# Retention attention and a Mish MLP on one core: state product on quarters of the array, scores moved behind the output ahead of them, state summed in SBUF, layer-2 tiles whole

## The chip, the cores and the metric

The kernel runs on one core of a Trainium2 chip. Times are device microseconds (us). "Time" is that of the whole execution; "span" is from the first to the last instruction in the profile and is about 1.7 us shorter. PE is TensorE's matmul side, PEld its weight loads, DVE is VectorE, ACT is ScalarE, POOL is GpSimd.

## The reference

```python
# q, k, v: (8, 8, 576, 64), that is batch, heads, sequence, head size
gamma  = 1.0 - 2.0 ** (-5.0 - np.arange(H))
Dmat   = np.where(rel >= 0, gamma[:, None, None] ** rel, 0.0)     # rel = i - j
ret    = (q @ k.T / sqrt(D)) * Dmat @ v
x      = ret.transpose(0, 2, 1, 3).reshape(4608, 512)
h      = x @ w_in                                                 # 512 -> 2048
out    = (h * tanh(softplus(h))) @ w_out                          # Mish, 2048 -> 512
```

Attention without a softmax can be done in chunks: within 128 positions by masked scores, across chunks by a state, the sum of k times v of all earlier positions (64 by 64 a head).

## The kernel before

There are 36 chunks of 128 positions in 18 pairs; four chunks make one of nine token tiles, 0 to 8, for the MLP. Pairs 0 and 1 and the chunks 4 to 7 (pairs 2 and 3) are handled chunk by chunk while the loads come in; pairs 4 to 7 with transposes on PE among the first layer-2 work; from pair 8 on DMA transposes q and k, and the rhythm is steady. The parts that the argument touches:

```python
ps_sc = ... bufs=2   # scores, 2 banks each     ps_st = ... bufs=1   # running state
ps_h  = ... bufs=2   # layer 1                  ps_o  = ... bufs=1   # layer 2

def step_k(m):       # add this pair to the state, which stays in PSUM
    ...
        nc.tensor.matmul(st[ds(64 * e, 64), u, p, :], lhsT=ks[:, u, h, :], rhs=vs[:, u, h, :], ...)
    for e in range(2):                       # two casts: a block-diagonal copy, zeros beside each head
        nc.scalar.activation(ssb[:, :, :, e, :], st, AX.Copy, scale=diag[:, e:e + 1])

def step_o(n):
    ot = sc[:, 0]
    ...      # across: 128 rows deep, half of them zeros, 64 columns
        nc.tensor.matmul(ot[ds(64 * e, 64), p, ...], lhsT=st_sb[b, i0][:, p, e, :], rhs=qk[:, 0, u, p, ...], ...)
    ...      # within: v times masked scores
        nc.tensor.matmul(ot[ds(64 * e, 64), p, :], lhsT=vs[:, u, 2 * p + e, :], rhs=sm[:, e, p, :], ...)
    (nc.scalar.copy if t == 0 else nc.vector.tensor_copy)(xts[t][:, :, ts(s, P)], ot)

# steady loop, 8 steps a pair: step 0 scores, step 4 state and outputs; g1 = 4 matmuls, g2 part = 4 matmuls
            if w == 0:   one(n, "S"); one(n + 1, "S"); step_p(m + 1); step_v(m + 1)
            elif w == 4: step_k(m); one(n, "O"); one(n + 1, "O")
            g1(t, i)
            g2(t - 1, i)
```

## Time and profile before

| | before |
|---|---|
| time, median of the first 3 runs | 317.01 us (316.92 to 317.5) |
| span of the profiled run | 315.1 us |
| PE busy | 97% |
| 512-column layer-1 and layer-2 matmuls | 496 and 560, 0.216 us each where they follow one another |
| a pair of chunks in the steady part | 15.84 us, 2.03 of them attention |

PE is the bound, so the way to read this profile is to ask what PE's own stream is made of. It helps to cut the span at three instructions: the first 512-column layer-1 matmul, the first layer-2 (G2) matmul, and the first layer-1 matmul of token tile 2. Here is the busy time of each engine in the four stretches, in the order start, chunk by chunk, PE transposes, rest. The columns are the stretch, its length, and the busy time of PE, PEld, DVE, ACT and POOL.

```profile
core 0: us, PE busy (x) PEld busy (x) DVE busy (x) ACT busy (x) POOL busy (x), PEclk, DMA share, GB/s
0.00:23.94 23.94, 19.52 (x159) 9.38 (x160) 14.44 (x35) 12.14 (x23) 20.13 (x36) 1.00 0.81 182
23.94:58.36 34.42, 33.31 (x497) 25.26 (x498) 13.77 (x18) 22.82 (x37) 21.25 (x23) 1.00 1.36 212
58.36:85.91 27.55, 27.36 (x276) 14.25 (x274) 15.28 (x17) 8.23 (x11) 11.93 (x13) 1.00 1.45 224
85.91:315.10 229.19, 225.71 (x1713) 110.26 (x1711) 90.74 (x103) 83.11 (x137) 30.89 (x37) 1.00 0.60 112
```

The reader is to see that the last stretch is three quarters of the time and nearly all PE, and that in the second ACT is busy for two thirds (22.82 of 34.42): there other engines are not far from setting the pace.

### The profile page before, as it was taken

The numbers are of one execution on the slowest core, as the hardware profiler recorded it, in microseconds if no ns is written. First come the engines' busy times: TensorE is split into PE (matmuls) and PEld (weight loads), VectorE is DVE, ScalarE is ACT, GpSimd is POOL, SyncE is SP. The second block draws the span as 40 slices with busy tenths as digits, with TensorE's granted clock in tenths as the row PEclk, the third lists the DMA queues.
The fourth block names the chain that finished last, engine by engine and source line by source line (L and its number), as shares of the span: only waits on it lengthen the run. The fifth ranks groups of instructions, "written<-read, shape, count | busy, mean of one in ns | idle before, by whom it ended". The sixth has DMA issues, their size and how long they took to land.

```text
span 315.1 us, 6075 instructions
## 1 busy us (share of the span) xinstructions
PE 305.9 (97%) x2639; PEld 159.2 (51%) x2639; DVE 134.2 (43%) x173; ACT 126.3 (40%) x208; POOL 84.2 (27%) x106
## 2 busy tenths in 40 slices
PE   7899999999999999999999999999999999999995
PEld 2355589645555544444545454445454545444444
DVE  4932463048649282626262626262626232001011
ACT  4556666322455642343434343434343432333300
POOL 6897672543340403131404040500000000000000
PEclk9999999999999999999999999999999999999999
DMA  6899999999999695959797969793131400000032
GB/s 170 240 134 219 206 205 220 201 229 253 198 251 166 127 132 108 197 110 201 158 141 157 142 139 160 165 149 87 46 89 45 91 33 35 33 33 35 33 83 83
DMA packets 71946, 43.38 MB, mean 138 GB/s; under 512 B 55664, under 2 KB 63088, under 8 KB 71920
## 3 DMA queue, kind: packets, MB, share of 16 engines
q0 software_dynamic: 43424, 26.22, 55.8%
q1 hardware_dynamic: 28352, 16.65, 20.4%
q8 instruction: 20, 0.33, 0.5%
q10 hardware_dynamic: 144, 0.13, 0.1%
q14 instruction: 6, 0.05, 0.0%
HBM read 36.70 MB, written 9.44 MB: 146 GB/s over the span
## 4 chain that ended last, share of the span: by engine, by line
PE 91%; DVE 4%; ACT 1%; DMA 1%; SPq 1%; issue 1%; DVEq 0%
PE hp L369 34%; PE ops L407 32%; PE hp L407 6%; PE hp L392 4%; PE sc L305 3%; PE sc L354 3%; PE sc L347 2%; PE st L326 2%; DVE qks L236 2%; PE sc L284 2%; PE hp L419 1%; DVE sm L308 1%; DMA qraw<-in_q_dram 1%; SPq L138 1%; ACT qkT L285 1%; PE hp L380 1%
## 5 line engine op out<-in xcount | busy, mean ns | idle before, releaser
L369 PE MATMUL hp<-xT,w_in_t 128*128 128x512 bf16 x496 | 126.5, 380 | 0.7 <-ACT gT L394 0.7
L371 ACT ACTIVATE gT<-hp 128x512 bf16<-128x512 f32 x124 | 74.1, 598 | 126.9 <-PE hp L369 126.6
L407 PE MATMUL ops<-w_out_t,gT 128*128 128x512 bf16 x480 | 121.9, 379 | 0.0
L407 PEld LDWEIGHTS <-gT 128*128 128x128 bf16 x560 | 54.2, 98 | 64.7 <-issue 0.8
L427 DVE COPY res<-ops 128x512 f32<-128x512 f32 x30 | 20.8, 692 | 128.0 <-PE ops L407 128.0
L369 PEld LDWEIGHTS <-w_in_t 128*128 128x128 bf16 x496 | 46.0, 98 | 53.8 <-DMA w_in_t<-in_moe_w_in_dram 0.8
L308 DVE TENSOR_TENSOR sm<-sc,mask 128x1024 bf16<-128x1024 f32 x36 | 42.6, 1217 | 20.2 <-PE sc L305 20.2
L540 POOL COPY seen<-qkT 1x1 bf16<-1x1 bf16 x10 | 1.8, 177 | 124.9 <-DMA qkT<-qks 124.9
L330 ACT ACTIVATE ssb<-st,diag 128x512 bf16<-128x512 f32 x32 | 20.2, 684 | 15.3 <-PE st L326 15.3
L358 DVE CAST xT<-sc 128x512 bf16<-128x512 f32 x32 | 20.8, 686 | 5.3 <-PE sc L354 4.5
L107 POOL DMA_DIRECT2D qraw<-in_q_dram x16 | 17.2, 1076 | 15.2 <-DVE qks L240 7.1
L257 DVE TENSOR_TENSOR vs<-vraw,gv 128x1024 bf16<-128x1024 f32 (+1 forms) x18 | 19.8, 1101 | 0.0
L240 DVE TENSOR_TENSOR qks<-qraw,gq 128x1024 bf16<-128x1024 f32 (+1 forms) x18 | 19.7, 1097 | 0.0
L107 POOL DMA_DIRECT2D qks<-in_k_dram x16 | 17.2, 1079 | 8.3 <-DMA qraw<-in_q_dram 3.8
L107 POOL DMA_DIRECT2D vraw<-in_v_dram x16 | 17.3, 1087 | 6.3 <-DMA w_out_t<-in_moe_w_out_dram 2.2
L407 PE MATMUL hp<-w_out_t,gT 128*128 128x512 bf16 x80 | 18.8, 380 | 0.0
L285 ACT COPY qkT<-sc 128x1024 bf16<-128x1024 bf16 x12 | 12.1, 1014 | 11.7 <-PE sc L284 11.7
L392 PE MATMUL hp<-xT,w_in_t 128*128 128x128 bf16 x272 | 16.7, 220 | 0.0
L392 PEld LDWEIGHTS <-w_in_t 128*128 128x128 bf16 x272 | 15.4, 98 | 0.7 <-issue 0.2
L354 PE MATMUL sc<-sm,vs 128*64 128x128 bf16 x288 | 13.9, 220 | 0.6 <-DVE sm L308 0.5
L305 PEld LDWEIGHTS <-qkT 64*128 64x128 bf16 x288 | 8.1, 94 | 10.2 <-issue 5.5
L305 PE MATMUL sc<-qkT 64*128 64x128 bf16 x288 | 11.9, 218 | 1.3 <-ACT qkT L285 0.8
(68 smaller groups left out, 157.1 us busy)
## 6 DMA issues: line engine op xcount, KB each, us to landing
out_dram<-res SPq DMA_DIRECT2D x31, 256.0 KB, 3.1
qraw<-in_q_dram POOLq DMA_DIRECT2D x12, 512.0 KB, 8.2
vraw<-in_v_dram POOLq DMA_DIRECT2D x12, 512.0 KB, 9.3
vraw<-in_v_dram POOLq DMA_DIRECT2D x12, 256.0 KB, 7.3
qks<-in_k_dram POOLq DMA_DIRECT2D x12, 256.0 KB, 8.5
qraw<-in_q_dram POOLq DMA_DIRECT2D x8, 256.0 KB, 9.4
w_out_t<-in_moe_w_out_dram POOLq DMA_DIRECT2D x4, 512.0 KB, 12.0
qraw<-in_q_dram SPq DMA_DIRECT2D x8, 128.0 KB, 4.0
```

What stands on the lines that cost most here:

```text
L107: nc.gpsimd.dma_start(out=t[ds(off, ni)].rearrange("p u h d -> p (u h) d"), in_=src[ds(b, 2), :, ds(i0, ni), :].rearrange("b h p d -> p (b ...
L257: (nc.gpsimd if early else nc.vector).tensor_tensor(r["vs"][:, u], r["v"][:, u], g, op=OP.mult)
L305: nc.tensor.matmul(sc[:, e, p, :], lhsT=qk[r, 1, u, p, :], rhs=qk[r, 0, u, p, :], start=True, stop=True)
L308: nc.vector.tensor_tensor(sm.rearrange("p e n i -> p (e n) i"), sc.rearrange("p e n i -> p (e n) i"), (mask if len(chunks[n]) == 1 else ma ...
L330: nc.scalar.activation(ssb[:, :, :, e, :], st, AX.Copy, scale=diag[:, e:e + 1])
L354: nc.tensor.matmul(ot[ds(64 * e, 64), p, :], lhsT=vs[:, u, 2 * p + e, :], rhs=sm[:, e, p, :], start=(start and p == 0), stop=True, skip_gr ...
L358: (nc.scalar.copy if t == 0 else nc.vector.tensor_copy)(xts[t][:, :, ts(s, P)], ot)
L369: nc.tensor.matmul(hp, lhsT=w_in_t[:, c, ts(f, P)], rhs=xts[t][:, c, :], start=(c == 0), stop=(c == KC - 1))
L371: nc.scalar.activation(gts[t][:, f, :], hp, AX.Mish)
L392: nc.tensor.matmul(hp[:, j, :], lhsT=w_in_t[:, c, ts(4 * fb + j, P)], rhs=xts[t][:, c, ts(s, P)], start=(c == 0), stop=(c == KC - 1))
L407: nc.tensor.matmul(ops, lhsT=gts[t][:, f, ts(s, P)], rhs=w_out_t[:, f, :], start=(f == 0), stop=(f == nF - 1))
L427: copy(ot, ops)
```

## The change

The intent: make PE's attention work shorter. The state product uses 64 by 64 quarters of the array, four at once; the scores of the next pair follow the output of the pair ahead, so that PE leaves its full shape once a pair and not twice. Three two-bank tiles for the scores make that possible, so the banks of the running state and of layer 2 go: the state is summed in SBUF by DVE, and a layer-2 tile is computed whole, in the banks of layer 1. Heads are regrouped (h and h + 4 share rows), and the decay moves from v to k, as DVE must now reorder k in any case.

```diff
-    ps_sc = ... bufs=2    ps_st = ... bufs=1    ps_o = ... bufs=1
+    ps_sc = ... bufs=3
 def step_p(m, ...):                       # DVE, once for each chunk
-        qks[:, 0] = q * gq                # k came by DMA as bf16; step_v: vs = v * gv
+        qks[:, 0] = q * gq;  qks[:, 1] = k * gk      # v comes by DMA as bf16
 def step_k(m):
+        if m < 6: st = ps_sc.tile(...)    else: st = ps_h.tile(...)
+        nc.vector.tensor_tensor(st_sum[b], st_sum[b], st, op=OP.add)      # or a copy, for the first
-        for e in range(2): nc.scalar.activation(ssb[..., e, :], st, AX.Copy, scale=diag[:, e:e + 1])
+        nc.scalar.copy(ssb, st_sum[b])
 def across(n, ot):
-        nc.tensor.matmul(ot[ds(64 * e, 64), p, ...], lhsT=st_sb[b, i0][:, p, e, :], rhs=qk[:, 0, u, p, ...])
+        r, p = ds(64 * e, 64), 2 * g + c
+        nc.tensor.matmul(ot[ds(64 * c, 64), e, g, ...], lhsT=st_sb[b, i0][r, p, :], rhs=qk[r, 0, u, p, ...])
 def step_o(n):                            # single chunks
-        (nc.scalar.copy if t == 0 else nc.vector.tensor_copy)(xts...)
+        within(...); across(...); nc.scalar.copy(xt...)
+def pair_o(m):                            # both chunks into the second one's score tile
+        step_k(m); within(u=0); within(u=1); across(u=0); across(u=1)
+        nc.vector.tensor_copy(xt..., sc...)          # one copy, 128x1024
 # steady loop
-            if w == 0: scores(m) ...   elif w == 4: step_k(m); outputs(m)
-            g1(t, i); g2(t - 1, i)
+            g1(t, i)
+            if i % 4 == 3:
+                if w == 7: pair_o(m); scores(m + 1)
+                for j in range(4): g2(t - 1, i - 3 + j)
```

Layer-2 tiles from token tile 2 on are copied out by ACT, and the transposes of pairs 6 and 7 by DVE.

More of the change, by code (lines that the diff above doesn't have):

```diff
@@ L75 @@
     PS = bass.MemoryType.PSUM
-    ps_sc = ctx.enter_context(tc.tile_pool(name="ps_sc", bufs=2, space=PS))
-    ps_st = ctx.enter_context(tc.tile_pool(name="ps_st", bufs=1, space=PS))
+    ps_sc = ctx.enter_context(tc.tile_pool(name="ps_sc", bufs=3, space=PS))
     ps_h = ctx.enter_context(tc.tile_pool(name="ps_h", bufs=2, space=PS))
-    ps_o = ctx.enter_context(tc.tile_pool(name="ps_o", bufs=1, space=PS))
     ctx.enter_context(tc.manual_schedule())
@@ L89, with by_slots @@
     w_out_r = moe_w_out.rearrange("(f p) d -> p f d", p=P)
+    def by_slots(x):
+        return x.rearrange("p (s r) d -> p r s d", r=2)
     def load(m):
@@ L93, in load @@
             return
-        qr = io.tile([P, 2, H, D], F32, name="qraw")
-        vr = io.tile([P, 2, H, D], F32, name="vraw")
-        qks = io.tile([P, 2, 2, H, D], BF16, name="qks", bufs=6)
-        pairs[m] = {"q": qr, "v": vr, "qks": qks, "ks": qks[:, 1]}
+        r = pairs[m] = {}
+        r["q"] = io.tile([P, 2, H, D], F32, name="qraw")
+        r["k"] = io.tile([P, 2, H, D], F32, name="kraw")
         if m < NCH // 2:
-            kr = io.tile([P, 2, H, D], F32, name="kraw", bufs=NCH // 2)
-            pairs[m]["k"] = kr
+            r["v"] = io.tile([P, 2, H, D], F32, name="vraw", bufs=NCH // 2)
             return
+        r["vs"] = tok.tile([P, 2, H, D], BF16, name="v", bufs=5)
         if m < NCH:
             return
-        for t, src in ((qr, q), (qks[:, 1], k), (vr, v)):
+        for x, src in (("q", q), ("k", k), ("vs", v)):
             off = 0
@@ L107, in load @@
                 nc.gpsimd.dma_start(
-                    out=t[ds(off, ni)].rearrange("p u h d -> p (u h) d"),
+                    out=r[x][ds(off, ni)].rearrange("p u h d -> p (u h) d"),
                     in_=src[ds(b, 2), :, ds(i0, ni), :].rearrange("b h p d -> p (b h) d"))
@@ L116, in load_single @@
         b, i0, _ = chunks[n][0]
-        r = pairs[m]
-        for t, src in ((r["q"], q), (r["qks"][:, 1], k), (r["v"], v)):
-            nc.gpsimd.dma_start(out=t[:, u], in_=src[b, :, ds(i0, P), :].rearrange("h p d -> p h d"))
+        for x, src in (("q", q), ("k", k), ("vs", v)):
+            nc.gpsimd.dma_start(out=pairs[m][x][:, u], in_=src[b, :, ds(i0, P), :].rearrange("h p d -> p h d"))
     def load_w_in(f, nf):
@@ L135, in load_first @@
         for x, src in (("q", q), ("k", k)):
-            heads = src.rearrange("b (p e) s d -> b e p s d", e=2)
+            heads = src.rearrange("b (e p) s d -> b e p s d", e=2)
             for e in range(2):
@@ L151, with scores_tile @@
     nc.vector.memset(idle, 0.0)
-    warm = ps_o.tile([P, d_model], F32, name="ops")
+    ahead = []
+    def scores_tile():
+        return ahead.pop() if ahead else ps_sc.tile([P, 2, NP, P], F32, name="sc")
     def keep_warm(n):
+        ahead.append(scores_tile())
         for _ in range(n):
-            nc.tensor.matmul(warm, lhsT=idle[:, 0:P], rhs=idle, start=True, stop=True)
+            nc.tensor.matmul(ahead[0][:, 0].rearrange("p n i -> p (n i)"), lhsT=idle[:, 0:P], rhs=idle, start=True, stop=True)
     keep_warm(11)
@@ L182 @@
             nc.vector.tensor_scalar(own[:, e, a:a + 1], off1, float(a),
-                                    math.log(1.0 - 2.0 ** (-5.0 - 2 * a - e)), op0=OP.is_equal, op1=OP.mult)
+                                    math.log(1.0 - 2.0 ** (-5.0 - a - 4 * e)), op0=OP.is_equal, op1=OP.mult)
     lg1 = consts.tile([P, 2], F32)
@@ L195 @@
     gq = consts.tile([P, 5, H], F32)
-    gv = consts.tile([P, 5, H], F32)
-    nc.scalar.activation(gv, ex, AX.Exp, scale=-1.0)
+    gk = consts.tile([P, 5, H], F32)
+    nc.scalar.activation(gk, ex, AX.Exp, scale=-1.0)
     nc.scalar.activation(gq, ex, AX.Exp)
@@ L210 @@
     load_v(1)
-    diag = consts.tile([P, 2], F32)
-    nc.vector.memset(diag, 0.0)
-    nc.vector.memset(diag[0:64, 0:1], 1.0)
-    nc.vector.memset(diag[64:P, 1:2], 1.0)
     seen = consts.tile([1, 1], BF16)
-    st_ps = {}
+    st_sum = {}
     st_sb = {}
@@ L229, in by_lines, with scale_first, cast_first @@
         return x.rearrange("p (t e) d -> p e t d", e=2)
-    def step_p(m, u0=0, nu=2):
+    def scale_first(n):
+        m, u = divmod(n, 2)
         r = pairs[m]
-        u = ds(u0, nu)
-        if m < NCH // 2:
-            nc.vector.tensor_tensor(by_lines(r["qks"][:, 0, u0]), by_heads(r["q"][:, u0]),
-                                    gq1.unsqueeze(3).to_broadcast([P, 2, 4, D]), op=OP.mult)
-            return
-        g = gq[:, place(2 * m), :].unsqueeze(1).unsqueeze(3).to_broadcast([P, nu, H, D])
-        nc.vector.tensor_tensor(r["qks"][:, 0, u], r["q"][:, u], g, op=OP.mult)
-    def step_c(n):
+        if u == 0:
+            r["qks"] = io.tile([P, 2, 2, H, D], BF16, name="qks")
+            r["vs"] = tok.tile([P, 2, H, D], BF16, name="v1", bufs=NCH // 2)
+        nc.vector.tensor_tensor(by_lines(r["qks"][:, 0, u]), by_heads(r["q"][:, u]),
+                                gq1.unsqueeze(3).to_broadcast([P, 2, 4, D]), op=OP.mult)
+    def cast_first(n):
         m, u = divmod(n, 2)
@@ L246, in step_c, with decay_first, step_p @@
         nc.gpsimd.tensor_copy(by_lines(r["qks"][:, 1, u]), by_heads(r["k"][:, u]))
-    def step_v(m, u0=0, nu=2):
+    def decay_first(n):
+        m, u = divmod(n, 2)
         r = pairs[m]
-        u = ds(u0, nu)
-        early = m < NCH // 2
-        if "vs" not in r:
-            r["vs"] = (tok.tile([P, 2, H, D], BF16, name="vs1", bufs=NCH // 2) if early
-                       else tok.tile([P, 2, H, D], BF16, name="vs"))
-        g = gv[:, place(2 * m), :].unsqueeze(1).unsqueeze(3).to_broadcast([P, nu, H, D])
-        (nc.gpsimd if early else nc.vector).tensor_tensor(r["vs"][:, u], r["v"][:, u], g, op=OP.mult)
+        nc.gpsimd.tensor_tensor(r["vs"][:, u], r["v"][:, u],
+                                gk[:, place(n), :].unsqueeze(2).to_broadcast([P, H, D]), op=OP.mult)
+    def step_p(m, us=(0, 1)):
+        r = pairs[m]
+        if "qks" not in r:
+            r["qks"] = io.tile([P, 2, 2, H, D], BF16, name="qks")
+            r["ks"] = r["qks"][:, 1]
+        for u in us:
+            for i, (x, g) in enumerate((("q", gq), ("k", gk))):
+                nc.vector.tensor_tensor(
+                    by_slots(r["qks"][:, i, u]), r[x][:, u].rearrange("p (r s) d -> p r s d", r=2),
+                    g[:, place(2 * m), :].rearrange("p (r s) -> p r s", r=2).unsqueeze(3).to_broadcast([P, 2, NP, D]),
+                    op=OP.mult)
     def step_t(n):
@@ L284, in step_t @@
                 nc.tensor.transpose(tp[:, i, p, :], flat[:, ts(p, P)], ident)
-        nc.scalar.copy(r["qk"][:, :, u], tp)
+        (nc.vector.tensor_copy if m in (6, 7) else nc.scalar.copy)(r["qk"][:, :, u], tp)
     def step_n(m):
@@ L300, in step_s @@
         qk = pairs[m]["qk"]
-        sc = ps_sc.tile([P, 2, NP, P], F32, name="sc")
+        sc = scores_tile()
         for p in range(NP):
@@ L318, in step_k @@
         ks, vs = pairs[m]["ks"], pairs[m]["vs"]
-        if i0 == 0:
-            st_ps[b] = ps_st.tile([P, 2, NP, 64], F32, name="st")
-        st = st_ps[b]
+        if m < 6:
+            st = ps_sc.tile([P, 2, 2, NP, 64], F32, name="sc")[:, 0]
+        else:
+            st = ps_h.tile([P, 2, NP, 64], F32, name="hp")
         for u in range(2):
@@ L324, in step_k, with within, across @@
                 for e in range(2):
-                    h = 2 * p + e
-                    nc.tensor.matmul(st[ds(64 * e, 64), u, p, :], lhsT=ks[:, u, h, :], rhs=vs[:, u, h, :],
-                                     start=(i0 == 0 and u == 0 and p == 0), stop=True, skip_group_check=True)
-        ssb = tr.tile([P, 2, NP, 2, 64], BF16, name="ssb", bufs=6)
-        for e in range(2):
-            nc.scalar.activation(ssb[:, :, :, e, :], st, AX.Copy, scale=diag[:, e:e + 1])
+                    nc.tensor.matmul(st[ds(64 * e, 64), u, p, :], lhsT=ks[:, u, 2 * p + e, :],
+                                     rhs=vs[:, u, 4 * e + p, :],
+                                     start=(u == 0 and p == 0), stop=True, skip_group_check=True)
+        if i0 == 0:
+            st_sum[b] = tr.tile([P, 2, NP, 64], F32, name="st")
+            nc.vector.tensor_copy(st_sum[b], st)
+        else:
+            nc.vector.tensor_tensor(st_sum[b], st_sum[b], st, op=OP.add)
+        ssb = tr.tile([P, 2, NP, 64], BF16, name="ssb", bufs=6)
+        nc.scalar.copy(ssb, st_sum[b])
         for u in range(2):
             st_sb[b + u, i0 + P] = ssb[:, u]
-    def step_o(n):
-        t, s = divmod(n, NCH)
+    def within(vs, sm, ot, start):
+        for h in range(H):
+            e, p = divmod(h, NP)
+            g, c = divmod(p, 2)
+            nc.tensor.matmul(ot[ds(64 * c, 64), e, g, :], lhsT=vs[:, h, :], rhs=sm[:, e, p, :],
+                             start=(start and g == 0), stop=True, skip_group_check=True)
+    def across(n, ot):
         m, u = divmod(n, 2)
-        qk, vs = pairs[m]["qk"], pairs[m]["vs"]
-        sc, sm = pairs[m][u]
-        ot = sc[:, 0]
-        start = True
+        qk = pairs[m]["qk"]
         off = 0
@@ L344, in step_o, with x_of @@
             if i0 > 0:
-                for p in range(NP):
+                for g in range(2):
                     for e in range(2):
-                        nc.tensor.matmul(ot[ds(64 * e, 64), p, ds(off, ni)], lhsT=st_sb[b, i0][:, p, e, :],
-                                         rhs=qk[:, 0, u, p, ds(off, ni)],
-                                         start=(start and p == 0), stop=False, skip_group_check=True)
-                start = False
+                        for c in range(2):
+                            r, p = ds(64 * e, 64), 2 * g + c
+                            nc.tensor.matmul(ot[ds(64 * c, 64), e, g, ds(off, ni)], lhsT=st_sb[b, i0][r, p, :],
+                                             rhs=qk[r, 0, u, p, ds(off, ni)],
+                                             start=False, stop=True, skip_group_check=True)
             off += ni
-        for p in range(NP):
-            for e in range(2):
-                nc.tensor.matmul(ot[ds(64 * e, 64), p, :], lhsT=vs[:, u, 2 * p + e, :], rhs=sm[:, e, p, :],
-                                 start=(start and p == 0), stop=True, skip_group_check=True)
+    def x_of(n):
+        t, s = divmod(n, NCH)
         if s == 0:
             xts[t] = xp.tile([P, KC, NCH * P], BF16, name="xT")
-        (nc.scalar.copy if t == 0 else nc.vector.tensor_copy)(xts[t][:, :, ts(s, P)], ot)
+        return xts[t], s
+    def step_o(n):
+        m, u = divmod(n, 2)
+        sc, sm = pairs[m][u]
+        ot = sc[:, :, 0:2, :]
+        within(pairs[m]["vs"][:, u], sm, ot, True)
+        across(n, ot)
+        xt, s = x_of(n)
+        nc.scalar.copy(xt[:, :, ts(s, P)].rearrange("p (e g) i -> p e g i", e=2), ot)
+    def pair_o(m):
+        sc = pairs[m][1][0]
+        ot = sc.rearrange("p e (g u) i -> p e g u i", g=2)
+        step_k(m)
+        for u in range(2):
+            within(pairs[m]["vs"][:, u], pairs[m][u][1], ot[:, :, :, u, :], u == 0)
+        for u in range(2):
+            across(2 * m + u, ot[:, :, :, u, :])
+        xt, s = x_of(2 * m)
+        nc.vector.tensor_copy(xt[:, :, ds(s * P, 2 * P)].rearrange("p n (u i) -> p n u i", u=2),
+                              sc.rearrange("p e (g u) i -> p (e g) u i", g=2))
     gts = {}
@@ L400, in g2 @@
         if part == 0:
-            if t == nT - 1 and s % 2 == 0 or (t, s) in ((0, 1), (0, 3), (1, 1)):
-                outs[t] = ps_h.tile([P, d_model], F32, name="hp")
-            else:
-                outs[t] = ps_o.tile([P, d_model], F32, name="ops")
+            outs[t] = ps_h.tile([P, d_model], F32, name="hp")
         ops = outs[t]
@@ L409, in g2 @@
         if part == 3:
-            store(t, s, ops, nc.vector.tensor_copy)
+            store(t, s, ops, nc.vector.tensor_copy if t < 2 else nc.scalar.copy)
     def g2_last(t, s):
@@ L437, in one @@
         for step in steps:
-            if step in "PV":
-                {"P": step_p, "V": step_v}[step](m, u, 1)
+            if step == "P":
+                step_p(m, (u,)) if n >= NCH else scale_first(n)
             else:
-                {"C": step_c, "T": step_t, "S": step_s, "O": step_o}[step](n)
+                {"C": cast_first, "V": decay_first, "T": step_t, "S": step_s, "O": step_o}[step](n)
     one(0, "PC")
@@ L462 @@
             one(n, "O")
+    ahead.clear()
     load_w_in(4, 4)
@@ L488 @@
         elif i == 12:
-            one(4, "PVT")
+            one(4, "PT")
         elif i == 14:
             one(4, "S")
-            one(5, "PV")
+            one(5, "P")
         elif i == 15:
@@ L506 @@
                 elif fb == 1 and n < 6:
-                    one(n + 2, "PV")
+                    one(n + 2, "P")
                 elif fb == 2:
@@ L519, in visit @@
             step_p(m)
-            step_v(m)
             if 2 * m + 2 < NPE:
@@ L531, in visit @@
             one(n + 1, "S")
-        elif w == 7:
-            step_k(m)
-            one(n, "O")
-            one(n + 1, "O")
+        elif w == 7 and m < 6:
+            pair_o(m)
     def cross(m):
@@ L540, in cross, with scores @@
         nc.gpsimd.tensor_copy(seen, pairs[m]["qk"][0:1, 0, 0, 0, 0:1])
+    def scores(m):
+        one(2 * m, "S")
+        one(2 * m + 1, "S")
     for i in range(nF):
@@ L554 @@
             step_p(8)
-            step_v(8)
         elif i == 8:
@@ L559 @@
         g1(2, i)
-        if i % 2:
-            g2(1, 8 + i // 2)
+        if i % 8 == 7:
+            pair_o(6 + i // 8)
+            if i == 15:
+                scores(8)
+            for j in range(4):
+                g2(1, 8 + i // 2 - 3 + j)
     for t in range(3, nT + 1):
@@ L565 @@
             m, w = 2 * (t + 1) + i // 8, i % 8
-            n = 2 * m
-            if m < n_pairs:
-                if w == 0:
-                    one(n, "S")
-                    one(n + 1, "S")
-                    if m + 1 < n_pairs:
-                        step_p(m + 1)
-                        step_v(m + 1)
-                elif w == 3:
-                    if m + 1 < n_pairs:
-                        cross(m + 1)
-                        load(m + 4)
-                elif w == 4:
-                    step_k(m)
-                    one(n, "O")
-                    one(n + 1, "O")
+            if m + 1 < n_pairs and w == 0:
+                step_p(m + 1)
+            elif m + 1 < n_pairs and w == 2:
+                cross(m + 1)
+                load(m + 4)
             if t < nT:
                 g1(t, i)
-            if t < nT or i < 12:
-                g2(t - 1, i)
+            if i % 4 == 3:
+                if m < n_pairs and w == 7:
+                    pair_o(m)
+                    if m + 1 < n_pairs:
+                        scores(m + 1)
+                for j in range(4):
+                    if t < nT or i < 12:
+                        g2(t - 1, i - 3 + j)
     g2_last(nT - 1, 1)
```

## The prediction

> **What bounds the kernel now.** I read the page first: the busy line, then the chain that ended last.
>
> ```profile
> PE 305.9 (97%) x2639; PEld 159.2 (51%) x2639; DVE 134.2 (43%) x173; ACT 126.3 (40%) x208; POOL 84.2 (27%) x106
> ...
> PE 91%; DVE 4%; ACT 1%; DMA 1%; SPq 1%; issue 1%; DVEq 0%
> ```
>
> TensorE (PE) is busy for 97% of the span and makes up 91% of the chain; no other engine passes 43%. Busy time of pipelined matmuls doesn't say how much of it is needed, so I next read the timeline of PE alone over one period of the steady part (start us, length us, line and operands).
>
> ```profile
> 221.45 1.03 PE L407 MATMUL ops<-w_out_t,gT 128*128 128x512 bf16 x4
> 222.41 0.62 PE L305 MATMUL sc<-qkT 64*128 64x128 bf16 x16
> 222.97 1.04 PE L369 MATMUL hp<-xT,w_in_t 128*128 128x512 bf16 x4
> ...
> 229.02 1.03 PE L407 MATMUL ops<-w_out_t,gT 128*128 128x512 bf16 x4
> 229.98 0.44 PE L326 MATMUL st<-vs,qks 128*64 128x64 bf16 x16
> 230.25 0.39 PE L347 MATMUL sc<-qkT,ssb 128*64 128x128 bf16 x8
> 230.48 0.39 PE L354 MATMUL sc<-sm,vs 128*64 128x128 bf16 x8
> 230.70 0.39 PE L347 MATMUL sc<-qkT,ssb 128*64 128x128 bf16 x8
> 230.92 0.39 PE L354 MATMUL sc<-sm,vs 128*64 128x128 bf16 x8
> 231.25 1.04 PE L369 MATMUL hp<-xT,w_in_t 128*128 128x512 bf16 x4
> ...
> 238.26 0.62 PE L305 MATMUL sc<-qkT 64*128 64x128 bf16 x16
> 238.81 1.04 PE L369 MATMUL hp<-xT,w_in_t 128*128 128x512 bf16 x4
> ```
>
> The reader is to see that PE never waits for another engine here, and that one pair of chunks costs 238.81 - 222.97 = 15.84 us. 64 of its matmuls are the two layers' 512-column ones: from 223.84 to 229.02 there are 24 of them in 5.18 us, 0.216 us each, so 64 take 13.81. The attention takes the other 2.03 us, in two visits. The score visit (L305): the full-width matmuls would have gone on at 221.45 + 4 x 0.216 = 222.31, and did at 222.97, so it costs 0.66. The output visit: 229.88 to 231.25, 1.37.
>
> Inside a visit I separate streams from boundaries. A last record lasts about 0.22 us (the groups' mean), so 16 scores start over 0.62 - 0.22 = 0.40 us, 0.027 each. The state's 16 matmuls (64 columns) start over 0.44 - 0.20 = 0.24 us, **0.016 each**. L347 and L354 use halves of the array's columns: 0.225 per eight, 0.028 each. What is left is the boundary where the tile shape changes: 222.41 - 222.31 = 0.10 on the way in, about 0.10 to 0.13 on the way out. The change from one small shape to another is in the trace too, earlier on:
>
> ```profile
> 49.83 0.40 PE L305 MATMUL sc<-qkT 64*128 64x128 bf16 x8 [0.25 <-ACT qkT L285]
> 50.15 0.44 PE L326 MATMUL st<-vs,qks 128*64 128x64 bf16 x16
> ```
>
> Eight scores take 8 x 0.027 = 0.22, but the state starts 0.32 after them: again **0.10 for a change of shape**, though nothing full-width is near.
>
> **What the Trainium skill says.** "TensorEngine Tiling (Array Packing)", Key Properties: changing the tiling mode drains TensorE, whereas tiles of one mode work side by side. The trace agrees: about 0.10 us at each change of shape, and none between L326 and L347, which share one (0.27 us for 16 x 0.016). The same page, Restrictions and Gotchas, says different row tiles must write different PSUM banks; the new kernel does that, as the row half picks the first index of a two-bank tile. No trace of before shows a violation. "TensorE: Matmul & The Clock Gate", section "Wait — 56ns, not 53.3ns?", gives a start-to-start floor of about 25 ns. The trace disagrees: 0.016 us for the state's small matmuls. So I take 16 ns as the floor for quarters.
>
> **The change part by part.**
> (1) *State product in quarters.* L347 had block-diagonal weights 128 rows deep, half of them zeros, on half the columns: two at a time. Now each is 64 by 64, four at a time. The number of matmuls stays. A 128-column stream takes 0.053 us of array (twice 0.027), a quarter of that is 0.013, so the issue floor of 0.016 binds: 8 x 0.016 = 0.13 per chunk in place of 0.225. There are 192 matmuls of this form, 24 chunks: 24 x 0.095 = **-2.3 us**. The other 64 records of L347 (64 columns, x16) are already at 0.016, so they gain nothing.
>
> (2) *Shape changes.* The quarter is a third small shape, so the visit "output, then state product" gets one more change, +0.10. In exchange the next pair's scores follow at once, so two visits become one. Per steady pair: before, in and out twice, 4 changes; after, full to columns, to quarters, to rows, to full, also 4. Counted over all: before, pairs 4 to 17 have 14 x 4 = 56. After: scores of 4 to 7 alone 8; outputs of 4 to 6 alone 9; outputs 7 to 16 with the next scores 4 each, less 2 for pairs 9 and 13, which start a sequence and have no state yet, 38; output 17 alone 3: 58. So +2, and the four single chunks 4 to 7 get one more each: +6 x 0.10 = **+0.6 us**. The merging alone just about pays for the new shape.
>
> (3) *State summed in SBUF.* Before, PSUM held the running sum and ScalarE wrote it twice with zeros, 2 x 0.68 us a pair. After, VectorE adds it in (about 0.69, as for its other 128x512 reads) and ScalarE casts once (about 0.6). Neither is on the path: a pair of chunks earlier is always time enough. 0.
>
> (4) *Decay moved from v to k, and heads regrouped.* Two 128x1024 operations of 1.22 us become four of 128x512, 0.69 each: VectorE +0.3 us a pair, off the path. Bytes loaded are the same (k as f32, v cast to bf16, the reverse of before). 0.
>
> (5) *G2 whole, two PSUM banks for both layers.* 16 matmuls of a kind in a row cost what four and four cost; no PE gain. But a layer-1 tile now gets its bank back after only one other tile, 8 x 0.216 = 1.73 us, in place of 3.5. That this fits is seen early in before, where L369 ran undisturbed, with the ScalarE lines of the same stretch:
>
> ```profile
> 29.64 2.75 PE L369 MATMUL hp<-xT,w_in_t 128*128 128x512 bf16 x12
> ...
> 30.70 0.60 ACT L371 ACTIVATE gT<-hp 128x512 bf16<-128x512 f32 x1 [0.41 <-PE hp L369]
> ```
>
> Twelve without a gap (11 x 0.216 + 0.38 = 2.75), on the same two banks. The read of the tile begun at 29.64 ended at 31.30, and its bank was wanted at 31.37: a margin of 0.07 us. G2's copy to ScalarE for the later tiles should take the same 0.60. So 0, but close.
>
> Sum: -2.3 + 0.6 = -1.7, from 317.0: **315.3 us**.
>
> **Rivals.** *Quarters don't overlap four deep* (weight loads or the drain bind, 0.027 each as now). For it: no run here shows four quarters at once. Against: the state's weight loads, 64 columns each too, keep pace at 0.016. Then only the +0.6 remains: 317.6. *Changes between small shapes are cheaper than 0.10 when the streams behind are short.* About 26 of the new count are of that kind; if free, another -2.6: 312.7. Against it stands the 0.10 at 50.15. *The bank turnaround becomes the wait.* The margin is 0.07 us, ScalarE has one more kind of work in that queue, and there are 112 layer-1 tiles from token tile 2 on; a tenth of a microsecond at every third is +3.7: about 319. For it: ScalarE is first come, first served. Against: the state's cast falls in the 3.5 us of a whole G2 tile, where no layer-1 tile waits. *The start decides*: the single chunks wait for ScalarE ("0.25 <-ACT qkT" above), and output casts there move onto ScalarE, while the doubled state write leaves it. I take this as up to half a microsecond either way.
>
> **Range and chances.** The main sum is two terms that I measured separately; the doubt is in the boundary (0.05 to 0.12 for each) and the floor for quarters (0.013 to 0.02): about a microsecond either way. The turnaround adds a tail upwards. I set 315.3, 8 in 10 between 313.6 and 317.0. Two per cent is 6.3 us. All of L347's 128-column stream is 24 x 0.225 = 5.4 us, so even a free state product would not reach it: faster 0.03. Slower needs a wait in most tiles: 0.02. Within 2%: 0.95.
>
> **What would show it.** Right: steady period near 15.65 us (15.84 - 0.19); x16 of the state product starting over 0.26 us in place of 0.45; gaps of about 0.10 on both sides of it; no wait of L369's successor on ScalarE; PE still 97%. Wrong: the quarter stream at 0.027 each (step 1); no gap at the new changes (step 2 too large); PE waiting for the Mish or the G2 copy in most periods (step 5); or the first 66 us, where attention runs chunk by chunk, moving by more than 0.5 us.

## The result

The time didn't move: 317.30 us median of 4 runs (317.27 to 317.33) against 317.08 (316.92 to 317.5). The ratio is 1.0005, with a 95% interval of 0.9987 to 1.0022. Ratios here are the mean time of one kernel's fast runs over that of the other's in the same rounds, so they are not quite the ratios of the medians quoted.

The page of the changed kernel, with the two lines that answer to those of before:

```profile
PE 303.8 (96%) x2639; PEld 157.5 (50%) x2639; DVE 127.5 (40%) x173; ACT 130.6 (41%) x219; POOL 83.8 (27%) x106
...
PE 86%; DVE 5%; ACT 3%; issue 2%; SPq 2%; DMA 1%; DVEq 0%
```

PE has 2.1 us less to do, yet the span is 0.5 us longer, and PE's share of the chain that ended last fell from 91 to 86%, while that of DVE and ACT together rose from 5 to 8%. So PE waits more. Where, the same four stretches tell, for the changed kernel:

```profile
0.00:24.53 24.53, 18.81 (x160) 9.24 (x161) 14.93 (x32) 11.54 (x22) 20.40 (x36) 1.00 0.84 183
24.53:59.89 35.36, 33.61 (x499) 25.08 (x497) 12.96 (x17) 23.52 (x39) 21.13 (x23) 1.00 1.34 213
59.89:88.29 28.40, 27.56 (x276) 14.06 (x274) 17.36 (x23) 6.30 (x8) 11.45 (x12) 1.00 1.40 219
88.29:315.60 227.31, 223.85 (x1712) 109.14 (x1711) 82.20 (x102) 89.22 (x150) 30.85 (x37) 1.00 0.58 111
```

The last stretch is 1.88 us shorter (227.31 against 229.19). The second is 0.94 longer, the third 0.85, the start 0.59. The gain was made and given back, all of it before 88 us.

PE's timeline over a steady pair shows that the mechanism works as meant:

```profile
219.02 0.44 PE L337 MATMUL hp<-v,qks 128*64 128x64 bf16 x16
219.30 0.62 PE L355 MATMUL sc<-sm,v 128*64 128x128 bf16 x16
219.84 0.42 PE L369 MATMUL sc<-qkT,ssb 64*64 64x128 bf16 x16
220.19 0.62 PE L315 MATMUL sc<-qkT 64*128 64x128 bf16 x16
220.75 3.63 PE L447 MATMUL hp<-w_out_t,gT 128*128 128x512 bf16 x16
...
236.42 3.63 PE L447 MATMUL hp<-w_out_t,gT 128*128 128x512 bf16 x16
```

A pair takes 236.42 - 220.75 = 15.67 us. The quarters (L369, shape 64*64) start 16 times over about 0.20 us, 0.013 each, even below the 0.016 that I had set as the floor. No line carries a wait.

The waits are in the second and third stretch. Two places, as the timeline of all engines shows them. First, after the state product of pair 2:

```profile
41.08 0.68 DVE L344 TENSOR_TENSOR st<-st,sc 128x512 f32<-128x512 f32 x1
...
41.79 0.62 ACT L346 CAST ssb<-st 128x512 bf16<-128x512 f32 x1 [1.85 <-DVE st L344]
...
42.31 1.08 ACT L437 ACTIVATE gT<-hp 128x512 bf16<-128x512 f32 x2
...
42.96 1.05 PE L435 MATMUL hp<-xT,w_in_t 128*128 128x128 bf16 x16 [0.22 <-ACT gT L437]
```

ACT stood 1.85 us for the sum on DVE, with a Mish (L437) behind it whose first tile had been ready for about 1 us (f1_defer, below, starts it at 41.04, with all of PE's work there 0.27 us earlier); then it had two to do, and PE waited for a bank. In the kernel before, the casts at this place followed PE's state product at once, and the Mish followed them:

```profile
39.35 1.27 ACT L330 ACTIVATE ssb<-st,diag 128x512 bf16<-128x512 f32 x2 [0.37 <-PE st L326]
40.51 1.33 ACT L394 ACTIVATE gT<-hp 128x512 bf16<-128x512 f32 x2
```

Second, in the third stretch, at the state product of pair 1:

```profile
80.34 0.68 DVE L342 COPY st<-sc 128x512 f32<-128x512 f32 x1
...
81.06 0.62 ACT L346 CAST ssb<-st 128x512 bf16<-128x512 f32 x1 [4.47 <-DVE st L342]
...
81.58 1.92 ACT L295 COPY qkT<-sc 128x1024 bf16<-128x1024 bf16 x2
...
83.56 0.40 PE L315 MATMUL sc<-qkT 64*128 64x128 bf16 x8 [0.42 <-ACT qkT L295]
```

The state came to DVE behind four operations of q and k, the cast waited for it, and two copies of transposes waited behind the cast, the first with its input (transposed from 79.15) long ready.

### The profile page after: what moved, and what is told of

The parts are those of the page before. It is cut to its first block, busy times and chain, and to the rows that moved or that the text cites. A ratio compares the mean times of both kernels' runs of the same rounds, so it can differ in the third digit from the quotient of the medians.

```text
span 315.6 us, 6091 instructions
## 1 busy us (share of the span) xinstructions
PE 303.8 (96%) x2639; PEld 157.5 (50%) x2639; DVE 127.5 (40%) x173; ACT 130.6 (41%) x219; POOL 83.8 (27%) x106
## 4 chain that ended last, share of the span: by engine, by line
PE 86%; DVE 5%; ACT 3%; issue 2%; SPq 2%; DMA 1%; DVEq 0%
PE hp L447 37%; PE hp L412 34%; PE hp L435 3%; PE sc L315 3%; PE sc L355 2%; SPq L141 2%; DVE qks L240 2%; ACT qkT L295 2%; DMA qraw<-in_q_dram 1%; PE sc L369 1%; PE sc L294 1%; PE hp L337 1%; PE hp L459 1%; DVE qks L264 1%; PE hp L423 1%
## 5 line engine op out<-in xcount | busy, mean ns | idle before, releaser
L447 PE MATMUL hp<-w_out_t,gT 128*128 128x512 bf16 x560 | 126.8, 379 | 0.0
L412 PE MATMUL hp<-xT,w_in_t 128*128 128x512 bf16 x496 | 113.9, 379 | 0.4 <-DVE xT L400 0.4
L467 ACT COPY res<-hp 128x512 f32<-128x512 f32 x27 | 15.8, 585 | 84.9 <-PE hp L447 84.9
L400 DVE CAST xT<-sc 128x1024 bf16<-128x1024 f32 x14 | 17.1, 1221 | 20.9 <-PE sc L369 20.5
L264 DVE TENSOR_TENSOR qks<-kraw,gk 128x512 bf16<-128x512 f32 x32 | 21.9, 683 | 0.0
L264 DVE TENSOR_TENSOR qks<-qraw,gq 128x512 bf16<-128x512 f32 x32 | 21.8, 681 | 0.0
L346 ACT CAST ssb<-st 128x512 bf16<-128x512 f32 x16 | 9.9, 618 | 23.7 <-DVE st L344 17.7
L111 POOL DMA_DIRECT2D v<-in_v_dram x16 | 17.3, 1081 | 5.4 <-DMA kraw<-in_k_dram 2.6
L111 POOL DMA_DIRECT2D kraw<-in_k_dram x16 | 17.1, 1072 | 5.5 <-issue 4.2
L315 PE MATMUL sc<-qkT 64*128 64x128 bf16 x288 | 12.0, 218 | 1.8 <-ACT qkT L295 1.2
L355 PE MATMUL sc<-sm,v 128*64 128x128 bf16 x288 | 12.0, 221 | 1.1 <-DVE sm L318 1.1
```

Of the source, the lines that this page charges most:

```text
L111: nc.gpsimd.dma_start(out=r[x][ds(off, ni)].rearrange("p u h d -> p (u h) d"), in_=src[ds(b, 2), :, ds(i0, ni), :].rearrange("b h p d -> p ...
L264: nc.vector.tensor_tensor(by_slots(r["qks"][:, i, u]), r[x][:, u].rearrange("p (r s) d -> p r s d", r=2), g[:, place(2 * m), :].rearrange( ...
L315: nc.tensor.matmul(sc[:, e, p, :], lhsT=qk[r, 1, u, p, :], rhs=qk[r, 0, u, p, :], start=True, stop=True)
L346: nc.scalar.copy(ssb, st_sum[b])
L355: nc.tensor.matmul(ot[ds(64 * c, 64), e, g, :], lhsT=vs[:, h, :], rhs=sm[:, e, p, :], start=(start and g == 0), stop=True, skip_group_chec ...
L400: nc.vector.tensor_copy(xt[:, :, ds(s * P, 2 * P)].rearrange("p n (u i) -> p n u i", u=2), sc.rearrange("p e (g u) i -> p (e g) u i", g=2))
```

## The experiments

Each kernel ran with a profile, and the stretches are read from it. Except for the start they turned out far more exact than times. "Rest" is the sum of the last three. In e1_heads and e3_order the profile is of an execution that took longer than the median, 320.74 and 319.42 us.

| run | start | second | third | last | rest | time, median |
|---|---|---|---|---|---|---|
| before | 23.94 | 34.42 | 27.55 | 229.19 | 291.16 | 317.08 |
| b_again | 24.23 | 34.42 | 27.55 | 229.20 | 291.17 | 317.08 (one run) |
| changed | 24.53 | 35.36 | 28.40 | 227.31 | 291.07 | 317.30 |
| e1_heads | 26.26 | 37.07 | 28.39 | 227.28 | 292.74 | 317.07 |
| e2_copydve | 24.15 | 35.37 | 28.40 | 227.28 | 291.05 | 316.93 |
| e3_order | 25.58 | 35.37 | 28.99 | 227.76 | 292.12 | 317.88 |
| e4_apart | 23.79 | 35.38 | 28.39 | 228.14 | 291.91 | 317.61 |
| g1_halves | 24.34 | 35.35 | 28.58 | 228.33 | 292.26 | 318.25 |
| f1_defer | 24.25 | 34.84 | 28.01 | 227.30 | 290.15 | 316.09 |
| f2_split | 24.35 | 34.83 | 27.49 | 227.73 | 290.05 | 316.10 |
| f3_all | 24.71 | 34.66 | 27.49 | 227.74 | 289.89 | 315.74 |
| h1_best | 24.57 | 34.66 | 30.51 | 225.46 | 290.63 | 316.58 |
| h2_fill | 24.61 | 35.37 | 31.32 | 225.50 | 292.19 | 318.50 (one run) |
| k1_three | 24.38 | 34.67 | 27.59 | 227.26 | 289.52 | 315.51 |

In h1_best and h2_fill one G2 tile of 3.45 us lies in the third stretch in place of the last; the rest is comparable.

**Is the reading sound? b_again** (the kernel before, unedited)

> The kernel before, unchanged, once more with a profile. Theory: its three stretches repeat within 0.1 us (34.42, 27.55 and 229.19), since nothing but PE's own order sets them; only the start to the first 512-column matmul (23.94) moves, by up to a microsecond, with the landing of the first loads. Rival: the stretches move too, then the differences of some tenths that I read from single profiles are noise.

The stretches repeated within 0.01 us. Differences of a tenth in the last three stretches can be read from single profiles; differences in the start can't.

**The scores apart again: e4_apart**

```diff
                     pair_o(m)
-                    if m + 1 < n_pairs: scores(m + 1)
                 for j in range(4): ... g2(t - 1, i - 3 + j)
+                if m + 1 < n_pairs and w == 7: scores(m + 1)
```

> The changed kernel with the next pair's scores after the whole G2 tile instead of right behind the output, in the nine steady pairs 9 to 17. Theory: PE pays one more in and out of the full shape and saves one change among the small ones, so a steady period of 15.67 becomes 15.78 to 15.80 us, and the time rises by 9 x 0.12 = 1.1 us to 318.4; the first 112 us are untouched. Rival: changes among the small shapes cost nothing extra, then +0.2 a pair, 319.2; or the merging was free, then 317.3.

The last stretch grew by 228.14 - 227.31 = 0.83 us, 0.09 for each of nine pairs; a steady pair took 15.77 us. This is the price of one more change of shape, nearer to my 0.12 than to either rival (0.2 and 0). So the merging pays, but little.

**Halves in place of quarters: g1_halves** Its output is wrong, which doesn't matter for the time.

```diff
-    lhsT=st_sb[b, i0][r, p, :], rhs=qk[r, 0, u, p, ds(off, ni)]
+    lhsT=st_sb[b, i0][:, p, :], rhs=qk[:, 0, u, p, ds(off, ni)]
```

> The changed kernel with the state product back on halves of the array (128 deep, both heads of a row pair summed: wrong result on purpose), all else the same, so the third small shape goes too. Theory: 16 matmuls start over 0.43 us in place of 0.21, and one change of shape of 0.10 goes: a steady period of 15.67 becomes 15.79, and from tile 2's layer 1 to the end 227.31 becomes about 228.6. Rival: the extra change of shape costs as much as the quarters save, then that stretch stays within 0.2 us; or the change is free, then 229.2.

The steady pair in its PE timeline:

```profile
235.67 0.62 PE L355 MATMUL sc<-sm,v 128*64 128x128 bf16 x16
236.12 0.61 PE L369 MATMUL sc<-qkT,ssb 128*64 128x128 bf16 x16
236.67 0.62 PE L315 MATMUL sc<-qkT 64*128 64x128 bf16 x16
```

The state product now lasts 0.61, not 0.42, and starts 0.45 after L355 in place of 0.54, as no change of shape lies between. The last stretch rose by 1.02 us, a pair by 0.10 (15.77). I had expected 1.3 and 0.12. From L369 to L315 it is 0.55 here and 0.35 with quarters: the quarters save about 0.20 a pair and pay about 0.10 of it for their own shape. Neither rival fits.

**The output copies of chunks 4 to 7 back on DVE: e2_copydve**

```diff
-        nc.scalar.copy(xt...)
+        (nc.scalar.copy if n < NCH else nc.vector.tensor_copy)(xt...)
```

> The changed kernel with the output copies of chunks 4 to 7 back on VectorE. Theory: ScalarE's copy there delays the Mish behind it, which PE waited for at 42.96 and 54.53 (0.22 and 0.21 us); both waits go, the first G2 tile starts at 59.45 in place of 59.89, time 316.9. Rival: the waits come from the later state cast and stay, or VectorE, now busier with k's decay, delays the transposes by as much: 317.3 or more.

My theory fell: PE still waited 0.22 for the Mish at 42.58 and at 54.16, and the second stretch is 35.37. The copy was not what delayed the Mish. What ACT waited for there was the state's sum, again 1.85 us. (The lower median comes from the start.)

**Two other orders: e3_order**

```diff
-            if m == 5: step_k(1)          # before the transposes of chunks 10 and 11
+        elif w == 4 and m == 5: step_k(1) # after them
 # pair_o: copy of the output first, then the state's sum and cast
```

> The changed kernel with two orders altered in the paired part: the second sequence's first state product goes after the transposes of chunks 10 and 11, and in every paired output the copy of the output stands before the state's sum on VectorE. Theory: the waits at 83.56 (0.42 us, scores on ScalarE's copy of the transposes, itself behind the state's cast) and at 88.29 (0.36, first layer-1 tile on the output copy behind the sum) go: layer 1 of tile 2 starts at 87.5 in place of 88.29, time 316.5. Rival: these waits only hide behind something else (loads), and the start of tile 2 moves by less than 0.2 us.

Also a miss: 28.99 and 227.76 us, both worse. The wait for the transposes' copy went, but PE, now sooner at the transposes of chunk 10, waited 0.43 and 0.21 there for DVE's q and k. The 0.36 at tile 2 stayed, so the sum ahead of the copy was not its cause: the copy alone takes 1.22 us, the G2 part between only 0.86. And behind the copy, the next bank wait for DVE (0.17 at the second layer-1 tile) was new.

**The state's cast later in ACT's queue: f1_defer**

```diff
 # chunk by chunk: step_k(n // 2) without its cast at the first of four parts ...
+                elif fb == 2: if n % 2 == 0: cast_k(n // 2)      # ... which comes two parts later
 # pair 1: the cast after the transposes
+        elif w == 4 and m == 5: cast_k(1)
```

> The changed kernel with ScalarE's cast of the state queued later where chunks or visits are short: after one more Mish for the products at chunks 4 and 6, after the transposes' copies for the second sequence's first product. Theory: the state's sum on VectorE makes the cast wait, and ScalarE, first come first served, holds the Mish and the transposes' copy behind it; so the waits of PE at 42.96, 54.53 and 83.56 go. From the first 512-column layer-1 matmul to the first G2 tile 34.76 us in place of 35.36, from there to tile 2's layer 1 27.80 in place of 28.40; time about 1.2 us less if the start is the same (316.1). Rival: the waits come from k's extra pass on VectorE; then both stretches stay.

This hit. The waits at 42.96, 54.53 and 83.56 are gone from the profile; the second stretch fell by 0.52 to 34.84, the third by 0.39 to 28.01 (0.60 expected of each), the last stayed. ACT at the first place:

```profile
41.04 0.60 ACT L443 ACTIVATE gT<-hp 128x512 bf16<-128x512 f32 x1 [1.36 <-PE hp L441]
41.93 0.60 ACT L443 ACTIVATE gT<-hp 128x512 bf16<-128x512 f32 x1 [0.29 <-PE hp L441]
42.43 0.61 ACT L352 CAST ssb<-st 128x512 bf16<-128x512 f32 x1
```

The third stretch gained 0.59 at the scores (from the first of them to layer 2, 82.74 to 83.89 before this edit, 81.93 to 82.49 now) and lost 0.2 again at pair 5's output, which k1_three explains. The time is 316.09 us, a ratio to before of 0.9966 (0.9950 to 0.9982). Only the place of one ScalarE instruction in its queue had changed, at three places.

**The output copy of pair 5 split between two engines: f2_split** (on top of the last)

```diff
+        for e, copy in enumerate((nc.scalar.copy, nc.vector.tensor_copy)): copy(xt[:, ds(2 * e, 2), ...], sc[:, ds(e, 1)]...)     # pair 5 alone
```

(The state's cast of pair 5 goes behind the copies too.)

> The same as the run with the later cast, and the output copy of the last pair before token tile 2 split between ScalarE and VectorE, a PSUM bank each. Theory: one copy of 1.22 us for both chunks, not the sum before it, makes layer 1 of tile 2 wait 0.36; split, it takes about 0.65, less than the 0.86 of the G2 part between, and the stretch from the first G2 tile to tile 2 falls by another 0.4 to 27.4. Rival: something behind it takes its place, less than 0.2 gained.

The third stretch fell by 0.52, the last rose by 0.43: the wait had moved on. The timeline of DVE says why:

```profile
86.53 0.69 DVE L408 CAST xT<-sc 128x512 bf16<-128x512 f32 x1 [0.88 <-ACT xT L408]
```

DVE's half waited for ACT's half, so the two ran one after the other, and layer 1 stopped after its first matmuls, which need only the first half. Why the halves are put in order, in two banks of one tile, I didn't find out.

**q and k of chunk 5 sooner on DVE: f3_all** (on top of both)

```diff
+        elif i == 13: one(5, "P")
         elif i == 14: one(4, "S")
-                      one(5, "P")
```

> The same, and the scaling of chunk 5's q and k queued one step earlier, ahead of the mask product of chunk 4. Theory: k's own pass on VectorE, new with the decay, makes the transposes of chunk 5 late by 0.38 us; moved ahead it is done in idle time: from the first 512-column matmul to the first G2 tile 34.4 in place of 34.76. All three together: span after the first 512-column matmul 289.1 in place of 291.07, time about 315.3, faster than both kernels by 0.5 to 0.6 per cent with usual starts. Rival: the loads of chunk 5 haven't landed by then, VectorE stands, and the mask product of chunk 4 is late: the stretch grows.

The second stretch fell by 0.17 to 34.66, not by 0.36. The transposes of chunk 5 no longer wait, but the output of chunk 4 now waits 0.57 us for its mask product in place of 0.35. DVE's timeline shows that it was the rival that came true:

```profile
35.33 0.69 DVE L264 TENSOR_TENSOR qks<-kraw,gk 128x512 bf16<-128x512 f32 x1 [0.59 <-DMA kraw<-in_k_dram]
35.94 1.22 DVE L318 TENSOR_TENSOR sm<-sc,mask 128x1024 bf16<-128x1024 f32 x1
```

DVE stood 0.59 us until chunk 5's k had landed, with the mask product of chunk 4 behind it: again one instruction that waits at the head of a queue.

**A G2 tile to hide the copy: h2_fill, and with three other orders h1_best**

```diff
+    visit(6, 0)
+    for j in range(4): g2(1, 8 + j)          # between pair 5's output and layer 1 of tile 2
 ...                                          # and no longer behind pair 6's output
 # h1_best also: f1's cast, f3's chunk 5, and
-        sc = pairs[m][1][0]
+        sc = pairs[m][0 if m < 6 else 1][0]
```

> The changed kernel with the moved G2 tile alone. Theory: the wait of 0.36 us at layer 1 of tile 2 goes and nothing takes its place: 290.7 us after the first 512-column matmul in place of 291.07. Rival: the wait shows up again within the next three microseconds.

> The changed kernel with four orders altered: the later cast of the state, chunk 5's scaling ahead of the mask product of chunk 4, the joint output of pairs 4 and 5 in the first chunk's tile (the second's must wait for both mask products), and one whole G2 tile moved from behind pair 6 to between pair 5's output and layer 1 of tile 2, where it hides the output copy. Theory: first stretch 34.7 us as in the run of all three; the waits of 0.19 at each of two outputs and of 0.36 at tile 2 go, so the rest, with the G2 tile counted where it now lies, is 291.07 - 0.7 - 0.6 - 0.2 - 0.36 - 0.38 = about 288.9 to 289.2 us after the first 512-column matmul; time about 315.0, some 0.6 per cent below before. Rival: as in the split copy, the wait moves on to the next layer-1 tile or to a transpose, and the rest stays near 289.9.

Another miss, in both. The wait of 0.36 went, but without the G2 tile behind pair 6 PE outran DVE. PE's timeline of h2_fill at that point:

```profile
102.46 1.02 PE L412 MATMUL hp<-xT,w_in_t 128*128 128x512 bf16 x4 [0.40 <-DVE st L344]
104.19 0.40 PE L294 MATMUL sc<-ident,qks 128*128 128x128 bf16 x4 [0.71 <-DVE qks L264]
104.80 0.40 PE L294 MATMUL sc<-ident,qks 128*128 128x128 bf16 x4 [0.21 <-DVE qks L264]
```

The rest is 1.12 us longer than in the changed kernel. The whole G2 tile had a worth where it stood: the time in which DVE caught up.

**The three orders that helped: k1_three** (f1's cast, f3's chunk 5, the joint output of pairs 4 and 5 in the first chunk's tile)

> The changed kernel with three orders altered and no G2 tile moved and no split copy: the later cast of the state, chunk 5's scaling one step earlier, the joint output of pairs 4 and 5 in the first chunk's tile. Theory: the stretches add up from the runs that measured each: 34.66 us to the first G2 tile, 28.01 - 0.38 = 27.63 to tile 2 (the wait of 0.36 there stays), 227.30 to the end, 289.6 together in place of 291.16 before; time about 315.4, 0.5 per cent below before with a usual start. Rival: the orders act on one another, and the sum stays above 290.

The rest is 289.52 us against 289.6 expected; the stretches add up. Against f1_defer the third stretch fell by 0.42 to 27.59, which is the joint tile's doing (chunk 5's order leaves this stretch alone: 27.49 in f2_split and f3_all). In the changed kernel the output of both chunks goes over the second chunk's scores, so even the first chunk's part can't start before the second mask product has read them. Pair 4's state product and output in f1_defer, then in k1_three:

```profile
73.90 0.44 PE L337 MATMUL sc<-v,qks 128*64 128x64 bf16 x16
74.36 0.64 PE L361 MATMUL sc<-sm,v 128*64 128x128 bf16 x16
...
73.86 0.44 PE L337 MATMUL sc<-v,qks 128*64 128x64 bf16 x16
74.13 0.62 PE L361 MATMUL sc<-sm,v 128*64 128x128 bf16 x16
```

The output starts 0.46 and 0.27 us after the state product, 0.19 late, and at pair 5 the same. In the changed kernel itself only pair 4 is late: at pair 5 (85.72 and 85.99, 0.27 apart) the wait at 83.56 had already given the mask product time. The time is 315.51 us, a ratio to before of 0.9961 (0.9942 to 0.9980): about 0.4% faster. With the changed kernel it shared no rounds; that one's ratio to before is 1.0005. Its stretches:

```profile
24.38:59.05 34.67, 33.33 (x497) 24.95 (x497) 13.06 (x17) 23.08 (x38) 20.77 (x22) 1.00 1.35 215
59.05:86.64 27.59, 27.19 (x276) 13.96 (x273) 17.38 (x23) 6.41 (x8) 12.07 (x13) 1.00 1.40 226
86.64:313.90 227.26, 223.86 (x1712) 109.10 (x1711) 82.25 (x102) 89.28 (x150) 30.82 (x37) 1.00 0.58 111
```

PE is busy 27.19 of 27.59 us in the third stretch, as good as before the change (27.36 of 27.55), and keeps the shorter last one.

**The first loads in the old order of heads: e1_heads** Its output is wrong, which doesn't matter for the time.

```diff
-            heads = src.rearrange("b (e p) s d -> b e p s d", e=2)
+            heads = src.rearrange("b (p e) s d -> b e p s d", e=2)
```

> The changed kernel with the first loads of q and k in the old order of heads (even and odd heads in place of first and second four); result wrong on purpose, work the same. Theory: the later landing of the second chunk's k (its cast began at 10.54 in place of 10.04 us) comes from the new pattern of the first loads, so the fourth chunk's output falls back from 21.89 to about 20.5 us, PE's first 512-column matmul from 24.53 to about 23.95 (there the weights' load sets it), and the time falls by about 0.6 us to 316.7. Rival: the landing has nothing to do with the pattern; the difference is how VectorE and GpSimd happen to meet, and time and markers stay within 0.15 us of the changed kernel's.

Inconclusive. The profile caught a long run of 320.74 us in which PE waited 2.10 us for w_in at 26.26, and the eight matmuls from there took 3.59 us in place of 1.90, which is the longer second stretch; its other runs took 316.46 to 317.30. The start also differs among kernels whose start is the same code: 23.79 (e4_apart), 24.15, 24.53, 25.58 (e3_order, 1.15 waited for w_in).

## Why the prediction was wrong

I said 315.3, with 313.6 to 317.0; it was 317.3.

**Steps (1) and (2), quarters and shapes: right, a little small.** For the last stretch they say 16 of the 24 chunks times 0.095, that is -1.5, with 48 changes of shape before and after. Measured -1.88. The 0.016 was not a floor, and calling the Trainium skill's floor of about 25 ns contradicted was a misreading (its page stands in the closing list). The start times in the trace of the changed kernel show two halves starting 3 ns apart, each again after 32 ns (219.076, 219.108, 219.139), so 16 ns is the mean over two halves. Four quarters with 128 columns start within 10 ns, each again after 56 ns (219.924, 219.980, 220.036), 14 ns each, which is the quarter stream of 0.013 that I had worked out and set aside. The 64-column ones, of which I expected nothing, start again after 32 ns (126.605, 126.637, 126.669), 8 ns each. g1_halves and e4_apart confirm both terms by taking them out. The rival "cheaper changes" is refuted: between L369 and L315 lie 0.35 us, of which 16 x 0.014 = 0.22 are the stream, so that change costs 0.13.

**Step (3), "Neither is on the path: a pair of chunks earlier is always time enough. 0": this failed.** It is true of the state's own reader, and I checked no other. The state's cast became the second link of a chain over two engines, and ACT, which takes its queue in order, stood still for it with a Mish or a copy behind it that PE needed. "PSUM — Partial Sum Buffer", section "Engine vs sequencer instructions", of the Trainium skill says that ScalarE's queue is strictly first in, first out; the trace agrees: ACT stood 1.85 us for the cast with a Mish queued behind it. f1_defer shows the size: 0.52 + 0.39 = 0.91 us, after the 0.2 that came back at pair 5. My rivals named ScalarE twice: its order, but for the steady part, where a whole G2 tile covers the cast, and not for the short steps, where nothing does; and, for the single chunks, the work that moves onto it, as half a microsecond either way, but not the wait at the head of its queue. Of my signs of being wrong the last came true: the first layer-2 matmul, before the 66 us that I named, moved from 58.36 to 59.89.

**Step (4), "VectorE +0.3 us a pair, off the path": failed too.** In the steady part it is right. Chunk by chunk the transposes need q and k, and k had come ready by DMA; now it waits for a pass of its own, where v's pass stood before. That cost 0.38 us at chunk 5 (from chunk 4's output to layer 1 behind the transposes 36.79 to 38.23, before 36.21 to 37.27); f3_all got 0.17 of it back, the other 0.2 is now a mask product that is late because DVE stands for k's landing.

**What I had not listed:** the joint output tile, which ties the first chunk's output to the second's mask product (0.42 us at two pairs, k1_three against f1_defer, half of it in the changed kernel, where only pair 4 is late), and the single copy of 1.22 us in place of two of 0.69, which layer 1 of tile 2 meets (0.36, read from the trace; both edits that took this wait away, the split copy and the moved G2 tile, brought others in its place). Both were in the diff. "TensorEngine Tiling (Array Packing)", section "PSUM Bottleneck", warns that tiling speeds up TensorE but not the evacuation of PSUM; the trace agrees: the start-to-start time of a pair's 16 state matmuls fell from 0.45 to 0.20 us, the copies of a pair's output take 1.29 before and 1.23 after, and PE waited for the copy.

**Step (5), the bank turnaround: right.** No steady period has a wait, so the small margin was enough.

**The sum.** With these orders mended, k1_three runs 291.16 - 289.52 = 1.64 us less than before over the last three stretches, where I had -1.7. The terms of PE were right in kind and the gain was there; the zeros were wrong, and in the changed kernel they cost 0.94 + 0.85 = 1.8 us. That -1.64 lies so near to -1.7 is partly luck: the last stretch gave -1.93 where I had -1.5, and the two before it cost 0.29 where I had about -0.2.

**The start** I gave half a microsecond either way. Two profiles of before have 23.94 and 24.23, the changed kernel 24.53, kernels with its start 23.79 to 24.71, two late ones 25.58 and 26.26. Three of 52 timed runs of the changed kernel and its variants took over 319 us, none of 34 of before. In the two of them that were profiled PE waited for w_in, but so it did, 1.03 us, in b_again. The profile of before is of a run of 316.78 us, 0.3 under the median; b_again has the median's time. Against b_again the changed kernel starts 0.30 later and has 0.10 less in the rest, which makes the +0.2 of the medians. Whether the change makes the start later stays open.

## What to carry to other kernels

When work moves to an engine that is "only 40% busy", look not at its share but at what stands behind the new instruction in its queue at the places where steps are short; a cast that waits for another engine holds up everything queued after it, and moving its place in the queue was about half of the cure here (0.91 of 1.8 us). Cut the span at instructions that all versions share and compare stretch by stretch: a change of zero was here -1.9 and +1.8. A piece of bound-engine work that seems to do nothing where it stands may be the time in which the others catch up, so moving it is not free.

## What the Trainium skill lacked or had wrong

- "TensorE: Matmul & The Clock Gate", section "Wait — 56ns, not 53.3ns?", has a floor of about 25 ns from start to start. The prediction calls it contradicted; it is not. The means here are 16 ns (64 columns on halves), 14 ns (128 on quarters) and 8 ns (64 on quarters), but each half or quarter starts its own matmuls 32 or 56 ns apart. Nothing to mend there.
- "TensorEngine Tiling (Array Packing)", Key Properties, says that a change of mode drains TensorE but gives no cost: 0.09 to 0.13 us for each change here, also between two small shapes, which for 16 matmuls of 128 columns is about half of what quarters save over halves (0.20 us).
- No page that I read has the cost of a wait at the head of a queue for the work behind it: 0.91 us in three places here, for a cast of 0.62 us at each that no one needed yet.
